# A retention and soft mixture-of-experts kernel on one core: the running maximum as a 129th column, a dispatch split in two, two scalings moved to GpSimd, and two more steps of k turned on the chip

## The chip, the cores and the metric

The kernel runs on one core of a Trainium2 chip. The metric is the device time of one execution in microseconds (us). An engine's work is named as in the profile: PE (TensorE, with PEld for its weight loads), DVE (VectorE), ACT (ScalarE), POOL (GpSimd), SP (SyncE, which issues all the DMAs here).

## The reference

Two layers follow each other. The first is a retention: per batch and head a 64x64 state decays by a factor of the head in each step of time and takes in k times v; the output is q times the state. The second is a soft mixture of 8 experts with 4 slots each: every slot takes a softmax over all 3072 tokens (dispatch), passes a two-layer network, and every token takes a softmax over the 32 slots (combine).

```python
for t in range(S):                                  # S = 768, 4 batches x 8 heads, head_dim 64
    state = gamma * state + k[t] outer v[t]
    y[t] = scale * (q[t] @ state)
x = y, as (3072 tokens, 512)
logits = x @ phi                                    # (3072, 32)
d = exp(logits - logits.max(0)); d /= d.sum(0) + 1e-9
slot_input = d.T @ x                                # (32, 512)
for e in range(8):
    h = maximum(slot_input[e] @ w1[e], 0)           # w1: 512 x 1024
    slot_out[e] = h @ w2[e]                         # w2: 1024 x 512
c = exp(logits - logits.max(1)); c /= c.sum(1) + 1e-9
out = c @ slot_out                                  # (3072, 512)
```

Everything is float32.

## The kernel before

**Attention in passes.** The sequence is cut into 6 chunks of 128 tokens; with 4 batches that makes 24 steps (`NSTEP`), step i being chunk i // 4 of batch i % 4. The loop at L437 makes 12 passes P of two steps each (`NPP`). A pass multiplies the carried state by q (`carry_mm`), the masked scores by v (`attend_mm`), copies the outputs out of PSUM (`attend_copy`), updates the state with k times v (`state_mm`, `state_add`), transposes the outputs to tokens x channels (`natural_mm`, `natural_copy`, the tile `xn`), and makes scores and masks of the next two steps (`score_mm`, `score_mask`). GpSimd multiplies the decays into q and v (`decay_q`, `decay_v`).

**Two layouts of k.** The scores need k with channels on the partitions, the state needs it with tokens on the partitions. The host lays down both, and a step's transfer brings kT, qT, v and the second layout of k, 1024 KB in all. For steps in `TURNED` (L46) and for the last four, the transfer stops ahead of the second layout (768 KB, L194), and for those in `TURNED` TensorE makes it by four transposes into bank A0, which ScalarE copies to the step's buffer (`turn_k`, L198 to L202; called at L487). A step of an even pass (P = 4) also has `turn_mm` and `turn_copy` of the dispatch behind it; a step of an odd pass has a dispatch and the logits.

**Dispatch by groups.** Four steps make a group g, one chunk of all batches, 6 groups in all. The logits of a group go to one PSUM bank "sm" as 128 partitions (4 batches x 32 slots) by 128 tokens (`logits_mm`). A running softmax over the tokens follows (`logits`): the maximum `m` so far, its negative `nm`, the exponentials `pT` with their sum `z`, and `al`, the factor by which what was summed before has to be scaled down. `pT` is transposed to `p`, and `dispatch_u` multiplies `p` by the `xn` of the group's four steps, into PSUM; `dispatch_acc` adds it to the accumulator `acc` (128 x 512) with the factor `al`, and `dispatch_z` does the same for the sums `zrun`.

**The turn to the experts** (L513 to L557) follows the last pass, in which the dispatch of group 4 (L475) and the first half of the logits of group 5 run ahead of `attend_mm`. Then: accumulate group 4, outputs and logits of the last steps, their maximum and exponentials (L522), the transposed `p` (L529), the factors `wj` that bring the four batches to one common maximum (L524 to L536, by way of a small matmul at L528), the dispatch of group 5 in two halves (L542), their accumulation, the division by the sums, and `siT`, the slots' inputs. `warm` (L409) multiplies zeros in the places where TensorE would wait. The first expert matmuls are those of L567.

**Order.** The order on every engine is the order of the code (`manual_schedule`). A wait for a buffer stands at its first writer.

**Buffers.** `ring` has 9 buffers of 512 KB: for the masked scores (two a pass), the transposed outputs and `xn` (one each a pass), and at P = 11 for four half-loads of w2 (L175). `inp` (6) holds the steps' inputs and `big` (13) weights; from P = 9 on weights go to `inp` too. All loads go through SyncE's one queue, and an issue whose buffer isn't free holds up the issues behind it. At L589 to L604 the last eleven weight loads are issued as the expert matmuls free buffers; the eight stores of L636 follow on the same queue.

**Experts.** `hidden` multiplies the slots' inputs by w1 (L567), L646 by w2 in three blocks of columns, and `finish` combines each block with the tokens' weights `cT` (L630), copies and stores it.

Of the kernel before, what the change touches and what calls it, by code (L numbers as in the profile page):

```python
# [11 lines left out]
AF = mybir.ActivationFunctionType  # L12
ALU = mybir.AluOpType
# [4 lines left out]
C = 128  # L18
# [24 lines left out]
NIN = 6  # L43
NRING = 9
PACE = (1, 1, 1, 2, 1, 2, 1, 2, 2, 0, 2, 2)
TURNED = (0, 1, 2, 3, 4, 8, 12)  # L46

K_MASK, K_VSC, K_YT = 0, 128, 176
K_ID, K_QT, K_GC, K_J, K_ALL = 272, 400, 496, 500, 504
# [32 lines left out]
def retention_soft_moe_kernel(  # L82
# [27 lines left out]
    def small(name, shape, bufs=1):  # L110
        return cpool.tile(shape, F32, name=name, bufs=bufs)

    def bank(name, shape=(128, 512)):
        return ps.tile(list(shape), F32, name=name)
# [190 lines left out]

    gs = {}

    def logits_mm(g, js):
        q = gs.setdefault(g, {})
        if "ltp" not in q:  # L310
            q["ltp"] = bank("sm", (128, C))
        for p in range(NPAIR):
            for j in js:
                nc.tensor.matmul(q["ltp"][32 * j:32 * j + 32, :], phis[:, p, :], st[GRP * g + j]["yT"][:, p, :],  # L314
                                 start=(p == 0), stop=(p == NPAIR - 1), skip_group_check=True,
                                 tile_position=(0, 32 * j))

    def logits(g):
        q = gs[g]
        lt = q["ltp"]  # L320
        q["pT"] = small("pT", [128, C])
        if g == NGRP - 1:
            nmx = small("nmx", [128, 1])
            nc.vector.tensor_reduce(nmx, lt, AX.X, ALU.max, negate=True)
            nc.vector.tensor_scalar(nmc[:, 1:2], nmx, nmc[:, 0:1], None, ALU.min)
            nc.scalar.activation(q["pT"], lt, AF.Exp, bias=nmc[:, 1:2], scale=1.0, accum_out=zc[:, 1:2])
            return
        nm = nmc[:, 0:1] if g == NGRP - 2 else small("nm", [128, 1])
        q["m"] = small("m", [128, 1], bufs=2)
        if g == 0:  # L330
            nc.vector.tensor_reduce(q["m"], lt, AX.X, ALU.max)
        else:
            mg = small("mg", [128, 1])
            nc.vector.tensor_reduce(mg, lt, AX.X, ALU.max)
            nc.vector.tensor_scalar(q["m"], mg, gs[g - 1]["m"], None, ALU.max)
        nc.vector.tensor_scalar(nm, q["m"], -1.0, None, ALU.mult)
        turn_l(g)
        q["z"] = zrun if g == 0 else small("z", [128, 1])
        nc.scalar.activation(q["pT"], lt, AF.Exp, bias=nm, scale=1.0, accum_out=q["z"])
        if g > 0:  # L340
            q["al"] = small("al", [128, 1])
            nc.scalar.activation(q["al"], gs[g - 1]["m"], AF.Exp, bias=nm, scale=1.0)

    def turn_l(g):
# [18 lines left out]
        q["p"] = small("pl", [128, C])  # L363
        nc.vector.tensor_copy(q["p"], pp)

    def dispatch_u(g, names):
        q = gs[g]
        q["up"] = [bank(n) for n in names]
        w = DM // len(names)
        for h, up in enumerate(q["up"]):  # L370
            for j in range(GRP):
                nc.tensor.matmul(up[32 * j:32 * j + 32, 0:w], q["p"][:, 32 * j:32 * j + 32],  # L372
                                 st[GRP * g + j]["xn"][:, h * w:(h + 1) * w], start=True, stop=True,
                                 skip_group_check=True, tile_position=(0, 32 * j))
# [2 lines left out]
        q = gs[g]  # L377
        nc.vector.scalar_tensor_tensor(zrun, zrun, q["al"], q["z"], ALU.mult, ALU.add)

    def dispatch_acc(g):  # L380
        q = gs[g]
        if g == 0:
            nc.scalar.copy(acc, q["up"][0])
            return
        w = DM // len(q["up"])
        for h, up in enumerate(q["up"]):
            a = acc[:, h * w:(h + 1) * w]
            nc.vector.scalar_tensor_tensor(a, a, q["al"], up[:, 0:w], ALU.mult, ALU.add)

    def combine_a(g):  # L390
        q = gs[g]
# [45 lines left out]
    for P in range(NPP):  # L437
# [34 lines left out]
            continue  # L472
        carry_mm(P)
        if last:
            dispatch_u(g - 1, ["A0"])  # L475
            logits_mm(g, (0, 1))
            load_halves(2)
            load_weights(2)
# [14 lines left out]
        if P % 2 == 1:  # L493
            if g > 0:
                dispatch_u(g - 1, ["S"])
            logits_mm(g, range(GRP))
            if g > 0:
                dispatch_acc(g - 1)
                combine_b(g - 1)
            if g > 1:  # L500
                dispatch_z(g - 1)
        score_mm(2 * P + 2)
        score_mask(2 * P + 2)
        score_mm(2 * P + 3)
# [7 lines left out]

    weight_pool[0] = big  # L513
    dispatch_z(g - 1)
    dispatch_acc(g - 1)
    attend_copy(NPP - 1)
    natural_mm(NPP - 1, (0,))
    combine_b(g - 1)
# [3 lines left out]
    logits(g)  # L522
    nj = small("nj", [128, GRP])
    nc.vector.tensor_scalar(nj, kt[:, K_J:K_J + GRP], nmc[:, 1:2], None, ALU.mult)  # L524
    natural_copy(NPP - 1, ("vector", "vector"), (1,))
    warm(2, "A0", 128)
    mb = bank("S", (128, GRP))
    nc.tensor.matmul(mb, rep, nj, start=True, stop=True)  # L528
    dispatch_p(g)  # L529
    al = gs[g]["al"] = small("al", [128, 1])  # L530
    nc.scalar.activation(al, gs[g - 1]["m"], AF.Exp, bias=nmc[:, 1:2], scale=1.0)
    warm(2, "A0", 128)
    nms = small("nms", [128, 1])
    nc.vector.tensor_reduce(nms, mb, AX.X, ALU.min)
    wj = small("wj", [128, 1])
    nc.scalar.activation(wj, nmc[:, 1:2], AF.Exp, bias=nms, scale=-1.0)  # L536
    gs[g]["z"] = zc[:, 1:2]
    dispatch_z(g)
    nc.vector.tensor_scalar(wsel, rep[:, 0:NSLOT], wj, None, ALU.mult)
    zw = small("zw", [128, 1])  # L540
    nc.vector.tensor_tensor(zw, zrun, wj, ALU.mult)
    dispatch_u(g, ["Y1", "A1"])  # L542
    dispatch_acc(g)
    zp = bank("S", (128, NSLOT))
    nc.tensor.matmul(zp, zw.broadcast_to([128, 128]), rep[:, 0:NSLOT], start=True, stop=True)
    sp = bank("A3", (128, NK * NSLOT)).rearrange("p (k s) -> p k s", s=NSLOT)
# [160 lines left out]
```

## Time and profile before

| | |
|---|---|
| median of three runs | 160.9 us (160.67 to 160.93) |
| the profiled execution | 160.49 us |
| its span, first to last instruction | 158.7 us |
| mean granted TensorE clock | 0.987 |
| DMA | 62.81 MB, of which 56.16 MB read and 6.29 MB written in HBM by the kernel's transfers |
| attention, to the end of the last `attend_mm` | about 101.7 us of the span |
| turn, to the first matmul of L567 | 101.7 to 107.9 us |
| experts and stores | 107.9 to 158.7 us |

The profile is of one execution. Its times run from the span's start. "The chain of waits" follows the work that ended last back from the end; a row of it gives start, length, engine, tile and line. A row of the timeline gives start and length of an instruction (or of several merged), its engine, line, what it writes and reads, and in brackets how long the engine had been idle and for whom it waited. A row of the windows gives a stretch, then busy time and count for PE, PEld, DVE, ACT and POOL, the granted clock, the DMA engines' mean busy share (1.00 is all 16), and GB/s. Rows of waits give the sum, the number of times and the longest. A DMA row gives the size and the time from issue to landing.

### The profile page before, as it was taken

What the parts mean: (1) busy time and instruction counts of PE and PEld (TensorE: products, weight loads), DVE (VectorE), ACT (ScalarE), POOL (GpSimd) and SP (SyncE); (2) the same over time, 40 slices, a digit from 0 to 9 for tenths busy, and PEclk for the clock granted to TensorE, in tenths of its full rate; (3) what the DMA queues carried; (4) which work ended last, traced back from release to release, by engine and by line L of the source; (5) the groups of instructions that cost most, each with busy time, mean ns of one, the idle gap of its engine ahead of it and who ended that gap; (6) DMA issues with size and microseconds to landing.
All of it is one profiled execution on the core that took longest, in us unless ns stands there. A gap on an engine that the chain in (4) does not pass through costs nothing.

```text
span 158.7 us, 5509 instructions
## 1 busy us (share of the span) xinstructions
PE 146.9 (93%) x2418; PEld 108.5 (68%) x2418; DVE 81.2 (51%) x201; ACT 39.8 (25%) x95; POOL 58.0 (37%) x62
## 2 busy tenths in 40 slices
PE   8899999999999999999999989999999999999700
PEld 2489989997998699979996867863233655556400
DVE  0347607592856385758574948488112304545510
ACT  3311552315142305130513051320101002424210
POOL 0352686965737377374738374000100000000000
PEclk9999999999999999999999999999999999999995
DMA  4999999999999999999999999999999999999991
GB/s 131 373 393 437 417 415 418 414 425 413 416 415 419 421 417 419 419 417 411 412 420 420 410 417 420 402 417 363 376 417 423 427 423 411 407 401 421 396 415 42
DMA packets 9816, 62.81 MB, mean 396 GB/s; under 512 B 1088, under 2 KB 1216, under 8 KB 4288
## 3 DMA queue, kind: packets, MB, share of 16 engines
q1 hardware_dynamic: 9792, 62.46, 96.4%
q8 instruction: 19, 0.31, 0.8%
q14 instruction: 5, 0.04, 0.1%
HBM read 56.16 MB, written 6.29 MB: 394 GB/s over the span
## 4 chain that ended last, share of the span: by engine, by line
PE 85%; DMA 3%; DVE 3%; issue 1%; ACT 1%; POOL 1%; SPq 0%; ACTq 0%; DVEq 0%
PE A L221 14%; PE Y L253 13%; PE A L646 9%; PE A L297 8%; PE S L281 6%; PE Y L244 6%; PE Y L567 4%; PE sm L314 4%; DMA r<-in_first_dram 3%; PE S L372 3%; PE A L567 2%; PE S L567 2%; PE A L630 2%; DVE r L228 2%; PE A L201 1%
## 5 line engine op out<-in xcount | busy, mean ns | idle before, releaser
L228 DVE TENSOR_TENSOR r<-A,kt 128x512 f32<-128x512 f32 x46 | 28.7, 684 | 18.8 <-PE A L221 18.8
L207 POOL TENSOR_TENSOR b<-b,qtab 128x512 f32<-128x512 f32 x20 | 25.5, 1276 | 24.5 <-DMA b<-in_x_dram 17.7
L221 PE MATMUL A<-b 64*128 64x128 f32 x384 | 25.2, 279 | 0.3 <-DMA b<-in_x_dram 0.3
L221 PEld LDWEIGHTS A<-b 64*128 64x128 f32 x384 | 22.5, 187 | 3.1 <-issue 2.2
L211 POOL TENSOR_TENSOR b<-b,kt 128x512 f32<-128x512 f32 x23 | 23.6, 1045 | 2.5 <-DMA b<-in_x_dram 2.5
L253 PE MATMUL Y<-r,b 128*64 128x128 f32 x352 | 22.3, 277 | 0.1
L253 PEld LDWEIGHTS Y<-r,b 128*64 128x64 f32 x352 | 19.0, 137 | 2.5 <-issue 2.3
L646 PE MATMUL A<-b,r 128*32 128x128 f32 (+1 forms) x352 | 15.9, 304 | 0.0
L646 PEld LDWEIGHTS A<-b,r 128*32 128x32 f32 x352 | 10.6, 110 | 7.1 <-issue 4.4
L304 ACT COPY r<-A 128x512 f32<-128x512 f32 x23 | 12.4, 591 | 9.4 <-PE A L297 9.4
L297 PE MATMUL A<-kt,r 128*128 128x128 f32 x96 | 13.2, 279 | 0.5 <-ACT r L272 0.5
L281 PE MATMUL S<-b 128*64 128x64 f32 x304 | 11.2, 222 | 0.8 <-issue 0.8
L297 PEld LDWEIGHTS A<-kt,r 128*128 128x128 f32 x96 | 10.4, 140 | 1.7 <-ACT r L272 0.7
L281 PEld LDWEIGHTS S<-b 128*64 128x64 f32 x304 | 10.6, 138 | 1.0 <-issue 1.0
L244 PE MATMUL Y<-b,sst 64*64 64x128 f32 x304 | 10.6, 276 | 0.0
L404 POOL TENSOR_TENSOR cn<-cn,cz 128x128 f32<-128x128 f32 x6 | 2.4, 399 | 20.4 <-DVE cz L403 14.9
L244 PEld LDWEIGHTS Y<-b,sst 64*64 64x64 f32 x304 | 8.2, 132 | 1.2
L273 DVE COPY r<-Y 128x512 f32<-128x512 f32 x9 | 6.2, 691 | 5.3 <-PE Y L253 4.5
L314 PEld LDWEIGHTS sm<-r,phis 128*32 128x32 f32 x192 | 6.2, 110 | 3.3 <-issue 3.3
L630 PE MATMUL A<-cT,r 32*128 32x384 f32 x26 | 8.3, 529 | 0.0
L567 PE MATMUL Y<-b,siT 128*32 128x512 f32 x64 | 8.2, 594 | 0.0
L290 DVE TENSOR_TENSOR sst<-sst,S 128x256 f32<-128x256 f32 x16 | 6.0, 417 | 3.1 <-PE S L281 3.1
(139 smaller groups left out, 177.8 us busy)
## 6 DMA issues: line engine op xcount, KB each, us to landing
b<-in_w_dram SPq DMA_DIRECT2D x30, 1024.0 KB, 14.7
b<-in_x_dram SPq DMA_DIRECT2D x13, 1024.0 KB, 12.5
b<-in_x_dram SPq DMA_DIRECT2D x10, 768.0 KB, 11.5
out_dram<-b SPq DMA_DIRECT2D x8, 768.0 KB, 9.0
r<-in_w_dram SPq DMA_DIRECT2D x4, 512.0 KB, 11.6
b<-in_x_dram SPq DMA_DIRECT2D x1, 512.0 KB, 4.3
r<-in_first_dram SPq DMA_DIRECT2D x1, 512.0 KB, 5.2
phis<-in_phi_dram SPq DMA_DIRECT2D x1, 64.0 KB, 9.4
```

The costliest lines, as they stand in the source:

```text
L207: nc.gpsimd.tensor_tensor(q, q, qtab, ALU.mult)
L211: nc.gpsimd.tensor_tensor(v, v, vsc[:, i // B, :].unsqueeze(2).broadcast_to([128, H, D]), ALU.mult)
L221: nc.tensor.matmul(s["sc"][r][:, g, :], s["kT"][half(r), g, :], s["qT"][half(r), g, :], start=True, stop=True, skip_group_check=True)
L228: nc.vector.tensor_tensor(s["A"][:, r], s["sc"][r], mask.unsqueeze(1).broadcast_to([128, NPAIR, C]), ALU.mult)
L244: nc.tensor.matmul(p["y"][k][b][half(half_of(r, g)), gl, :], sst[(2 * P + k) % B][half(r), g, :], s["qT"][half(r), g, :], start=(gl == 0 a ...
L253: nc.tensor.matmul(pr[P]["y"][k][g // 2][half(half_of(r, g)), g % 2, :], s["v"][:, 2 * g + r, :], s["A"][:, r, g, :], start=(P < B // 2 an ...
L281: nc.tensor.matmul(S_[half(r), k, g, :], s["kn"][:, 2 * g + r, :], s["v"][:, 2 * g + r, :], start=True, stop=True, skip_group_check=True)
L297: nc.tensor.transpose(X[k][:, g * 128:(g + 1) * 128], pr[P]["yT"][:, k, g, :], ident)
L304: (nc.scalar.copy if engines[k] == "scalar" else nc.vector.tensor_copy)(xn, pr[P]["X"][k])
L314: nc.tensor.matmul(q["ltp"][32 * j:32 * j + 32, :], phis[:, p, :], st[GRP * g + j]["yT"][:, p, :], start=(p == 0), stop=(p == NPAIR - 1), ...
L567: nc.tensor.matmul(hp[g][hf][32 * j:32 * j + 32, :], siT[:, k, :], w1t[4 * g + j, k][:, hf * 512:(hf + 1) * 512], start=(k == 0), stop=(k ...
L646: nc.tensor.matmul(op[32 * j:32 * j + 32, :w], hT[fc // 4][:, fc % 4, 4 * g + j, :], w2t[4 * g + j, cb, fc], start=(g == 0 and fc == 0), s ...
```

## The change

- `TURNED` also holds steps 10 and 16. Their transfers are 256 KB shorter each, and `turn_k` runs for them in passes 4 and 7.
- The logits' bank of the last group gets a 129th column, into which VectorE copies the running maximum `m` of group 4, in pass 10 (`logits_bank`). One reduction over 129 columns then gives the negative overall maximum `nmc[:, 1:2]`; the separate minimum goes.
- The dispatch of group 4 is split by columns: half 0 stays at its place in the last pass, half 1 stands in the turn, behind the copy of the last step's `xn`, where two products with zeros stood. Its accumulation is split likewise, the second part behind `dispatch_z(g)`.
- The last `natural_copy` goes from VectorE to ScalarE; `al` of the last group is computed earlier, and has two buffers.
- The second `warm` of the turn writes bank A2 in place of A0.
- `wsel` and `zw`, the scalings by `wj`, go from VectorE to GpSimd.

```diff
-TURNED = (0, 1, 2, 3, 4, 8, 12)
+TURNED = (0, 1, 2, 3, 4, 8, 10, 12, 16)
...
+    def logits_bank(g):
+        gs.setdefault(g, {})["ltm"] = bank("sm", (128, C + 1))
+        gs[g]["ltp"] = gs[g]["ltm"][:, 0:C]
+        if g == NGRP - 1:
+            nc.vector.tensor_copy(gs[g]["ltm"][:, C:C + 1], gs[g - 1]["m"])
...
-            nmx = small("nmx", [128, 1])
-            nc.vector.tensor_reduce(nmx, lt, AX.X, ALU.max, negate=True)
-            nc.vector.tensor_scalar(nmc[:, 1:2], nmx, nmc[:, 0:1], None, ALU.min)
+            nc.vector.tensor_reduce(nmc[:, 1:2], q["ltm"], AX.X, ALU.max, negate=True)
...
-    def dispatch_u(g, names):
+    def dispatch_u(g, names, hs=None):
...
-        for h, up in enumerate(q["up"]):
+        for h in range(len(names)) if hs is None else hs:
+            up = q.setdefault("up", {})[h] = bank(names[h])
...
         if last:
-            dispatch_u(g - 1, ["A0"])
+            dispatch_u(g - 1, ["A0", "A0"], (0,))
             logits_mm(g, (0, 1))
...
+        if P == NPP - 2:
+            logits_bank(NGRP - 1)
         score_mm(2 * P + 2)
...
     dispatch_z(g - 1)
-    dispatch_acc(g - 1)
+    dispatch_acc(g - 1, 2, (0,))
...
-    natural_copy(NPP - 1, ("vector", "vector"), (1,))
-    warm(2, "A0", 128)
+    al = gs[g]["al"] = small("al", [128, 1], 2)
+    nc.scalar.activation(al, gs[g - 1]["m"], AF.Exp, bias=nmc[:, 1:2], scale=1.0)
+    natural_copy(NPP - 1, ks=(1,))
+    dispatch_u(g - 1, ["A0", "A0"], (1,))
     mb = bank("S", (128, GRP))
     nc.tensor.matmul(mb, rep, nj, start=True, stop=True)
     dispatch_p(g)
-    al = gs[g]["al"] = small("al", [128, 1])
-    nc.scalar.activation(al, gs[g - 1]["m"], AF.Exp, bias=nmc[:, 1:2], scale=1.0)
-    warm(2, "A0", 128)
+    warm(2, "A2", 128)
...
     dispatch_z(g)
-    nc.vector.tensor_scalar(wsel, rep[:, 0:NSLOT], wj, None, ALU.mult)
+    dispatch_acc(g - 1, 2, (1,))
+    nc.gpsimd.tensor_scalar(wsel, rep[:, 0:NSLOT], wj, None, ALU.mult)
     zw = small("zw", [128, 1])
-    nc.vector.tensor_tensor(zw, zrun, wj, ALU.mult)
+    nc.gpsimd.tensor_tensor(zw, zrun, wj, ALU.mult)
     dispatch_u(g, ["Y1", "A1"])
-    dispatch_acc(g)
+    dispatch_acc(g, 2)
```

More of the change, by code (lines that the diff above doesn't have):

```diff
@@ L310, in logits_mm @@
         if "ltp" not in q:
-            q["ltp"] = bank("sm", (128, C))
+            logits_bank(g)
         for p in range(NPAIR):
@@ L340, in logits @@
         if g > 0:
-            q["al"] = small("al", [128, 1])
+            q["al"] = small("al", [128, 1], 2)
             nc.scalar.activation(q["al"], gs[g - 1]["m"], AF.Exp, bias=nm, scale=1.0)
@@ L364, in dispatch_p @@
         nc.vector.tensor_copy(q["p"], pp)
-    def dispatch_u(g, names):
+    def dispatch_u(g, names, hs=None):
         q = gs[g]
-        q["up"] = [bank(n) for n in names]
         w = DM // len(names)
-        for h, up in enumerate(q["up"]):
+        for h in range(len(names)) if hs is None else hs:
+            up = q.setdefault("up", {})[h] = bank(names[h])
             for j in range(GRP):
@@ L378, in dispatch_z, with dispatch_acc @@
         nc.vector.scalar_tensor_tensor(zrun, zrun, q["al"], q["z"], ALU.mult, ALU.add)
-    def dispatch_acc(g):
+    def dispatch_acc(g, n=1, hs=None):
         q = gs[g]
@@ L384, in dispatch_acc @@
             return
-        w = DM // len(q["up"])
-        for h, up in enumerate(q["up"]):
+        w = DM // n
+        for h in range(n) if hs is None else hs:
             a = acc[:, h * w:(h + 1) * w]
-            nc.vector.scalar_tensor_tensor(a, a, q["al"], up[:, 0:w], ALU.mult, ALU.add)
+            nc.vector.scalar_tensor_tensor(a, a, q["al"], q["up"][h][:, 0:w], ALU.mult, ALU.add)
     def combine_a(g):
```

## The prediction

> **What bounds the kernel now.** I read the chain of waits first, then SyncE's waits, then windows of half a microsecond over the two places where the DMA share sags, then the landing times of single transfers.
>
> ```profile
> PE 146.9 (93%) x2418; PEld 108.5 (68%) x2418; DVE 81.2 (51%) x201; ACT 39.8 (25%) x95; POOL 58.0 (37%) x62
> DMA  4999999999999999999999999999999999999991
> ...
> SPq L162 <- PE Y L567: 10.2, 4, 7.8
> ...
> SPq L702 <- DMA out_dram<-b: 5.7, 1, 5.7
> ```
>
> Two things are full at once: TensorE 93% of the span, and the DMA engines in every slice from the second to the last but one. The chain names PE almost throughout and no DMA after the first load. But after the last instruction of the computation SyncE waits another 5.7 us for the last store. So the last transfer ends the run, and the question is what fixes its time. The next fences give issue and landing of three transfers, each from a window that holds one issue.
>
> ```profile
> 101.73 0.33 SPq L162 DMA_DIRECT2D b<-in_w_dram  x1
> b<-in_w_dram SPq DMA_DIRECT2D x1, 1024.0 KB, 11.8
> 109.88 0.33 SPq L162 DMA_DIRECT2D b<-in_w_dram  x1
> b<-in_w_dram SPq DMA_DIRECT2D x1, 1024.0 KB, 6.1
> 151.55 0.33 SPq L636 DMA_DIRECT2D out_dram<-b  x1
> out_dram<-b SPq DMA_DIRECT2D x1, 768.0 KB, 6.1
> ```
>
> The last load before the turn lands at 101.73 + 11.8 = 113.5, the first one after it at 109.88 + 6.1 = 116.0, and the last store at 157.6, 1.1 before the end of the span. A transfer has landed when the slowest of the 16 engines is done, and at 417 GB/s (the usual rate of the GB/s row) 1024 KB take 2.5 us: 113.5 to 116.0 is just that. So the **slowest engine** goes from old to new load without a gap, although SyncE stood 7.8 us in between (its wait on Y L567, the first expert matmuls, which free weight buffers).
>
> ```profile
> 109.50:110.00 0.50, 0.50 (x8) 0.13 (x4) 0.36 (x1) 0.00 (x0) 0.00 (x0) 1.00 0.75 311
> 110.00:110.50 0.50, 0.50 (x8) 0.13 (x4) 0.48 (x1) 0.00 (x0) 0.00 (x0) 1.00 0.52 213
> ...
> 111.50:112.00 0.50, 0.50 (x12) 0.14 (x7) 0.00 (x0) 0.00 (x0) 0.37 (x1) 1.00 0.80 295
> 112.00:112.50 0.50, 0.50 (x8) 0.13 (x4) 0.31 (x1) 0.00 (x0) 0.03 (x1) 1.00 1.07 426
> ...
> 154.50:155.00 0.50, 0.00 (x0) 0.00 (x0) 0.00 (x0) 0.00 (x0) 0.00 (x0) 0.50 0.72 295
> 155.00:155.50 0.50, 0.00 (x0) 0.00 (x0) 0.00 (x0) 0.00 (x0) 0.00 (x0) 0.50 0.30 123
> ...
> 156.50:157.00 0.50, 0.00 (x0) 0.00 (x0) 0.00 (x0) 0.00 (x0) 0.00 (x0) 0.50 0.06 25
> ```
>
> The last two figures of a row are DMA share and GB/s. From 109.5 to 112 half of the engines are empty: they are ahead, ran dry, and wait for the issue at 109.88, whose data is flowing at about 111.7 (shares 0.80, then 1.07). At the end most engines stop near 155.0, and from 156 the share is 0.06, one engine of 16: it alone carries the end from 155.1 to 157.6, and nothing in the views shows it idle before. Its time is the sum of its bytes; the others' end hangs on when the weight buffers come free.
>
> **The change part by part.** *Two more steps turned.* Steps 10 and 16 load 768 instead of 1024 KB: 512 KB less in all, 512/1024 x 2.5 = **1.25 us** less for each engine, the slowest included, long before 113.5. In return TensorE transposes four blocks for each. A pass with a turned step against one without:
>
> ```profile
> 35.27 0.59 PE A L201 x4
> 35.86 0.87 PE A L297 x8
> ...
> 44.45 1.02 PE A L297 x8
> ...
> 97.90 1.00 PE A L372 x8
> 98.89 0.86 PE sm L314 x16
> ...
> 103.82 0.53 PE A L412 x4
> ...
> 105.37 0.49 PE Y L372 x8
> 105.86 0.43 PE A L372 x8
> 106.29 0.34 PE S L545 x2
> ```
>
> 0.59 + 0.87 - 1.02 = 0.44 us each, on the PE chain without cover: **+0.88 us**. (ScalarE's copy of a turned step, some 0.6 us, must leave bank A0 before the next scores: they follow the L201 by 0.87 us and more, so nothing.)
>
> *Half a dispatch.* The dispatch of group 4 at L475 takes 1.00 us for 512 columns; a half of 256 takes 0.43 to 0.49, say 0.46: -0.54. The other half takes the place of a warm-up of 0.53: -0.07. Together **-0.61 us**, if PE stays the path. It does: the last attends need masks that are done at 98.4, and the warm-up left in place covers exp, copy and minimum as before.
>
> *129th column.* L325 (0.21) goes.
>
> ```profile
> 95.21 0.28 ACT L357 COPY pl<-sm 128x128 f32<-128x128 f32 x1
> 95.88 2.48 DVE L228 TENSOR_TENSOR r<-A,kt 128x512 f32<-128x512 f32 x4 [2.16 <-PE A L221]
> ...
> 103.61 0.21 DVE L325 TENSOR_SCALAR nmc<-nmx,nmc 128x1 f32<-128x1 f32 x1
> 103.92 0.37 ACT L326 ACTIVATE pT<-sm,nmc 128x128 f32<-128x128 f32 x1 [1.00 <-PE A L297]
> 104.00 0.68 DVE L304 COPY r<-A 128x512 f32<-128x512 f32 x1
> 105.27 0.29 ACT L536 ACTIVATE wj<-nmc,nms 128x1 f32<-128x1 f32 x1 [0.71 <-DVE nms L534]
> ```
>
> Exp may start some 0.25 earlier, but TensorE runs fillers until 104.35, so it is worth nothing on the path. Its price is the copy of the maximum into the bank, of L325's size, on VectorE: it waits for L357 (until 95.49) and has 0.39 us before the masks at 95.88; if it is late, the masks' end at 98.4 still has over a microsecond before the attends at 99.75. Behind it on VectorE stand only these masks. Nothing.
>
> *Copy of step 23 to ScalarE.* Behind exp (from 103.92) and the moved `al` it would end near 105.1, less the 0.25: before the last dispatch at 105.37 and before wj at 105.27. Nothing. VectorE gives the 0.68 to the half accumulation, which stands before wj's users and ends before the first half of the last dispatch.
>
> *Scalings on GpSimd.* No row shows this operation.
>
> ```profile
> L404 POOL TENSOR_TENSOR cn<-cn,cz 128x128 f32<-128x128 f32 x6 | 2.4, 399 | 20.4 <-DVE cz L403 14.9 <-DVE zc L378 5.5
> L211 POOL TENSOR_TENSOR r<-r 128x512 f32<-128x512 f32 x1 | 1.5, 1547 | 6.0 <-DMA r<-in_first_dram 6.0
> L456 POOL COPY rep<-kt 32x128 f32<-32x128 f32 x4 | 1.1, 286 | 0.1
> L695 POOL MEMSET const-float32-0.0<- 128x1 f32 x1 | 0.1, 98 | 0.2 <-issue 0.2
> ```
>
> wj ends at 105.56, and TensorE is free for L545, which needs zw, at 106.29: 0.73 us for two operations and their hand-overs. Lowest 2 x 0.10, nearest 0.29 + 0.10 (128x32 and 128x1 are smaller than L404 and of L456's order), highest the first L211, twice: 3.1. I take 0.4 to 0.5 with hand-overs: covered, at most 0.1 on the path. The upper end is the slower rival below. [...]
>
> *Ring buffers.* The half held back keeps the two copies of group 4 until about 104.
>
> ```profile
> SPq L175 <- PE A L372: 3.7, 1, 3.7
> 98.92 0.33 SPq L175 DMA_DIRECT2D r<-in_w_dram  x1
> ```
>
> The fourth half-load waited for exactly that dispatch. Three buffers are free earlier; the next one in the order of the code is that of pair 10's outputs, free after L314 (99.75, less 0.54). So this issue moves by about 0.3, and those behind it on SyncE little, since they wait for the attends anyway. If instead it waited for the held half, 2.5 MB would come 5 us late; the slowest engine, busy until about 106 with what is queued, would lose some 0.9 of the 1.25.
>
> **The sum.** TensorE reaches the experts 0.88 - 0.61 = 0.27 us later, up to 0.4 with GpSimd. New data flows at 111.7 + 0.3 = 112.0; the slowest engine has finished old work at 113.5 - 1.25 = 112.25. It still has no gap, so all of the 1.25 should arrive at the end; the margin of 0.25 is thin, and I take **-1.2 us**. The next limit would be the others, 155.1 + 0.3 = 155.4, still below 157.6 - 1.2 = 156.4. The profiled execution took 160.49 with a span of 158.7; it becomes 159.3 with 157.5. The median of the three runs, 160.9, lies 0.4 above it: **159.7**.
>
> **The rivals.**
> *Only the restart counts* (0.16). If the end hangs on the release of weight buffers alone, the bytes saved before it only lengthen the hole at 110, and the time moves with TensorE: +0.3, 161.2. For it: half the engines do run dry there. Against it: 113.5 and 116.0 with no gap. The laggard is made by something, and the trace has 19 packets of instructions on a queue of their own:
>
> ```profile
> q8 instruction: 19, 0.31, 0.8%
> ```
>
> [...]
> *GpSimd becomes the path* (0.14, the slower side). Place: L545 and L548 behind wsel and zw. It turns the sign once the pair costs more than 0.73 + 1.5 = 2.2, since that much is swallowed first by the cover and then by the 1.5 us between 113.5 and 112.0. At the highest row, 3.1, TensorE is 0.3 + 2.4 = 2.7 late and the end 2.7 - 1.8 = 0.9 later: 161.8.
> *The turn isn't shorter* (0.12): the held half or a ring buffer gives back the 0.6, or the fourth half-load waits. TensorE 0.9 late, or the engine 0.9 idle: 0.3 to 0.9 gained, 160.3.
> *The laggard vanishes* (0.06): another engine fetches the instructions late; then the others' limit counts, -2.2: 158.7.
>
> **How the numbers follow.** The forecast has 0.52. Faster by over 0.2% (0.32 us, about what a measurement of this kernel can tell from none): 0.52 + 0.12 + 0.06 = 0.70. Only the restart is 0.11 within and 0.05 beyond; with GpSimd slower is 0.19. The range leaves out the vanished laggard and the dear GpSimd pair, 0.20: from 159.1 (forecast, less the lower runs and noise of 0.3 to 0.6) to 161.3 (restart alone).
>
> **What would show it.** Right: the last load before the turn lands about 1.25 after less queue (near 112.3), the first after it 2.5 later, the hole at 110 wider, one engine still alone at the end, last store landing near 156.4; L201 in passes 4 and 7, L372 of 0.46 twice, first L567 at about 108.2. Wrong: the last load at 112 and the next at 116 or later (restart), L545 waiting for GpSimd, L175's last issue after 104, or TensorE waiting for a bank at the second half dispatch.

## The result and the profile after

| | before | after |
|---|---|---|
| median (5 runs each, side by side) | 160.67 us | 162.55 us (161.91 to 163.19) |
| ratio, 95% interval | | 1.0121 [1.0081, 1.0161] |
| the profiled execution, its span | 160.49, 158.7 | 161.91, 160.1 |
| first expert matmul starts | 108.07 | 110.37 |
| from there to the end of the span | 50.6 | 49.8 |
| last store issued, landed | 151.55, 157.6 | 153.85, 159.0 |

The forecast was 159.7 (159.1 to 161.3), faster; it is 1.9 us slower. From a kernel's runs the comparisons leave out those more than 1.5% above its fastest as disturbed, and the profiled execution of the run called e5 below is one of these and isn't read.

Two rows of the page of after, TensorE and the DMA share in 40 slices:

```profile
PE 147.5 (92%) x2430; PEld 109.2 (68%) x2430; DVE 81.0 (51%) x199; ACT 41.2 (26%) x98; POOL 58.5 (37%) x64
...
DMA  4999999999999999999999978999899999999992
```

TensorE has more to do and a smaller share; the DMA engines, without a gap before, sag at the slices 24, 25 and 29.

In the profiled executions the end moves by 1.4: TensorE reaches the experts 2.3 us later, where 0.27 was forecast, and 0.9 of it comes back behind. First the chain of waits of after (start, length, what). It covers the two turned steps of passes 4 and 7, the turn, and a kind of row that the prediction did not use: "issue", time in which the engine waits for nothing that the profile shows.

```profile
44.49 0.59 PE A L201 x4
45.08 0.87 PE A L297 x8
...
51.73 0.77 issue
...
59.65 0.07 issue
...
69.54 0.59 PE A L201 x4
...
85.51 0.66 issue
...
93.01 0.79 issue
...
100.57 0.57 PE A L376 x8
...
106.06 0.57 PE A L376 x8
```

The same rows in the chain of before, with its first expert matmul:

```profile
51.37 0.55 issue
...
84.28 0.22 issue
...
108.07 0.93 PE A L567 x8
```

The turned steps and the two halves stand there as the change has them. What is new is 0.77 + 0.07 + 0.66 + 0.79 = 2.29 us of "issue" in the attention, against 0.55 + 0.22 = 0.77 before: **1.5 of the 2.3**. The turned steps add 0.88, the shorter turn takes 0.37, and some 0.3 is left to waits between engines in the last passes.

What these gaps are shows in the timeline of TensorE in after, around the one at 85.5, and in the DMA view of the stretch 83.5 to 84.0 (a queue, its packets and MB):

```profile
84.70 0.80 PE L281 MATMUL S<-b 128*64 128x64 f32 x21
86.17 0.56 PE L281 MATMUL S<-b 128*64 128x64 f32 x11 [0.66 <-issue]
...
q8 instruction: 1, 0.02, 13.5%
```

A run of 32 equal matmuls of `state_mm` is torn after the 21st. Nothing in these lines of the code asks for a stop there. Counted through TensorE's instructions in the trace, weight loads included, the gaps of before stand at number 1729 and 3009, those of after at 1729, 1985, 3009 and 3265: all are 193 + 256k, though the code at a number is another in part. The same holds for every gap over 0.1 us of the runs below, those in which the code is moved against the count included. Ahead of each lies one packet of 16 KB on queue q8, the kind "instruction" (19 of them, 0.31 MB, in the page of before). In after one starts at 83.72 and takes 1.08 us; TensorE goes on 1.4 us behind its end, at 86.17. So TensorE's program comes in **blocks of 256 instructions**, and at these places the next block isn't there yet. A block lasts 5.7 to 7 us in the attention. The fetch of the next block starts only some 3 to 5 us after the end of the block ahead, that is, after TensorE has entered the block in hand (in after 4.7, 4.9, 5.0 and 5.2 us at the four with gaps), so that with 1.1 for the packet and 1.4 behind it the block is just on hand or just not.

The DMA engines lose too. Windows of after (last two figures: share, GB/s), then two waits and three issues of SyncE, each issue with its row of size and time to landing:

```profile
92.00:94.00 2.00, 1.21 (x31) 0.79 (x25) 1.93 (x7) 0.00 (x0) 1.92 (x3) 1.00 0.79 324
94.00:96.00 2.00, 1.76 (x30) 1.52 (x27) 0.58 (x3) 1.23 (x4) 1.40 (x2) 1.00 0.68 201
96.00:98.00 2.00, 1.88 (x19) 1.47 (x21) 0.40 (x1) 1.07 (x3) 0.00 (x0) 1.00 0.83 299
...
112.00:114.00 2.00, 2.00 (x24) 0.62 (x20) 1.57 (x5) 0.00 (x0) 0.06 (x1) 1.00 0.69 205
```
```profile
SPq L159 <- PE Y L253: 7.7, 1, 7.7
...
SPq L175 <- PE sm L320: 3.6, 1, 3.6
```
```profile
103.98 0.33 SPq L162 DMA_DIRECT2D b<-in_w_dram  x1
b<-in_w_dram SPq DMA_DIRECT2D x1, 1024.0 KB, 10.5
112.18 0.33 SPq L162 DMA_DIRECT2D b<-in_w_dram  x1
b<-in_w_dram SPq DMA_DIRECT2D x1, 1024.0 KB, 5.1
153.85 0.33 SPq L643 DMA_DIRECT2D out_dram<-b  x1
out_dram<-b SPq DMA_DIRECT2D x1, 768.0 KB, 5.2
```

The load that waits for `attend_mm` of pass 10 (L253) is issued at 94.86 in place of 92.18, and from 92 to 98 the share sags to 0.68; before it was 1.00 to 1.02 there. So the engines now run dry at two places. The last load ahead of the turn lands at 103.98 + 10.5 = 114.5, the next one at 112.18 + 5.1 = 117.3: 2.8 later, where 2.5 would be without a gap.

Of the two places the first costs more. The load issued at 86.80 still lands at 97.1 (10.3 us later); in before the same load was issued at 84.90 and landed at 98.5 (13.6 us later). So at 97 us after is 1.4 ahead, the saved bytes in full. At the last load ahead of the turn it is 0.9 behind (114.5 against 113.5): 2.3 us are lost there, and 0.3 at the turn.

### The profile page after: what moved, and what is told of

Read it like the earlier page. It is cut to its first block, busy times and chain, and to the rows that moved or that the text cites. A ratio compares the mean times of both kernels' runs of the same rounds, so it can differ in the third digit from the quotient of the medians.

```text
span 160.1 us, 5542 instructions
## 1 busy us (share of the span) xinstructions
PE 147.5 (92%) x2430; PEld 109.2 (68%) x2430; DVE 81.0 (51%) x199; ACT 41.2 (26%) x98; POOL 58.5 (37%) x64
## 4 chain that ended last, share of the span: by engine, by line
PE 87%; DMA 3%; issue 2%; DVE 1%; POOL 1%; ACT 1%; SPq 0%; DVEq 0%
PE A L221 14%; PE Y L253 14%; PE A L653 9%; PE A L297 7%; PE Y L244 6%; PE S L281 6%; PE Y L574 4%; PE sm L320 4%; DMA r<-in_first_dram 3%; PE S L376 2%; PE A L574 2%; PE S L574 2%; PE A L201 2%; PE A L637 2%; PE sm L637 1%
## 5 line engine op out<-in xcount | busy, mean ns | idle before, releaser
L253 PE MATMUL Y<-r,b 128*64 128x128 f32 x352 | 22.6, 276 | 0.9 <-issue 0.8
L253 PEld LDWEIGHTS Y<-r,b 128*64 128x64 f32 x352 | 19.2, 137 | 3.4 <-issue 3.3
L304 ACT COPY r<-A 128x512 f32<-128x512 f32 x24 | 13.0, 592 | 8.2 <-PE A L297 8.2
L297 PEld LDWEIGHTS A<-kt,r 128*128 128x128 f32 x96 | 10.5, 140 | 1.7 <-ACT r L272 0.7
L320 PEld LDWEIGHTS sm<-r,phis 128*32 128x32 f32 x192 | 6.2, 110 | 2.9 <-issue 2.7
```

The source lines that it names most:

```text
L253: nc.tensor.matmul(pr[P]["y"][k][g // 2][half(half_of(r, g)), g % 2, :], s["v"][:, 2 * g + r, :], s["A"][:, r, g, :], start=(P < B // 2 an ...
L297: nc.tensor.transpose(X[k][:, g * 128:(g + 1) * 128], pr[P]["yT"][:, k, g, :], ident)
L304: (nc.scalar.copy if engines[k] == "scalar" else nc.vector.tensor_copy)(xn, pr[P]["X"][k])
```

## The experiments

All times are medians of all runs of a kernel. The ratio is to the kernel before, run beside it, whose medians lie between 160.46 and 160.78; where a text below takes differences of medians, a few tenths are within that scatter. "Idle" sums the pieces of "issue" over 0.06 us in the attention of the profiled execution, "experts" is the start of the first expert matmul there.

| run | what it is | us | ratio, 95% interval | idle | experts |
|---|---|---|---|---|---|
| before | | 160.67 | 1 | 0.77 | 108.07 |
| after | | 162.55 | 1.0121 [1.0081, 1.0161] | 2.29 | 110.37 |
| e1 | before + turned steps | 163.18 | 1.0155 [1.0115, 1.0195] | 2.68 | 111.41 |
| e2 | before + the rest | 160.39 | 0.9988 [0.9966, 1.0011] | 1.16 | 107.92 |
| e3 | after + 116 at the start | 160.94 | 1.0027 [0.9998, 1.0056] | 0.27 | 108.41 |
| e4 | after, 15 loads fewer | 157.13 | one run | 0 | 107.15 |
| e5 | before + 124 at the start | 160.67 | 1.0013 [0.9985, 1.0041] | | |
| e6 | e2 + 124 at the start | 160.44 | 0.9984 [0.9956, 1.0012] | 1.10 | 108.17 |
| e7 | e1 with whole loads | 163.47 | 1.0178 [1.0129, 1.0228] | 3.03 | 111.82 |
| e8 | before + 32 idle in passes 4, 7 | 162.68 | 1.0119 [1.0077, 1.0162] | 1.88 | 109.74 |
| e9 | before, 512 KB fewer | 160.39 | 0.9989 [0.9966, 1.0012] | 1.17 | 108.81 |
| e10 | before + 32 idle in the last pass | 160.79 | 1.0020 [0.9992, 1.0048] | 1.56 | 109.48 |
| e11 | e2 + step 6 turned | 162.15 | 1.0120 [1.0076, 1.0164] | 2.54 | 110.27 |
| e12 | after + 124 at the start | 160.94 | 0.9988 [0.9962, 1.0013] | 1.00 | 108.99 |
| e13 | after + 240 at the start | 161.80 | 1.0045 [1.0009, 1.0080] | 1.16 | 109.37 |
| e14 | before + 16 at the start | see there | 0.9954 [0.9916, 0.9992] | 1.51 | 108.59 |
| e15 | e2 + 512 KB fewer | 159.80 | 0.9953 [0.9933, 0.9974] | 1.17 | 108.44 |
| e16 | after + 64 at the start | 158.39 | 0.9878 [0.9846, 0.9910] | 0 | 107.02 |
| e17 | after + 184 at the start | 160.53 | 0.9985 [0.9956, 1.0015] | 0 | 107.99 |
| e18 | before + 64 at the start | 159.83 | 0.9960 [0.9939, 0.9980] | 0 | 107.35 |

The numbers "at the start" are TensorE instructions, four for each small product with zeros (16 of them take the pages' count of products from 2430 in after to 2462 in e16, and that of weight loads likewise), in the stretch where TensorE waits for the first loads anyway (its first product with data starts at 5.11 in before).

### Which half of the change, and is it the fetch (e1 to e4)

e1 is before with the new `TURNED` alone, e2 is after with the old one, e3 and e4 are after with one edit each:

```diff
 e3
-    warm(WARM)
+    warm(2)
+    warm(32, "sm", 8)
 e4, in the weight loads
-            t = large(weight_pool[0])
+            if which == "w1" and (e, k) != (0, 0):
+                t = one[0]
+            else:
+                t = large(weight_pool[0])
...
-                nc.sync.dma_start(t, w1[e // 2, k])
+                if (e, k) == (0, 0):
+                    one.append(t)
+                    nc.sync.dma_start(t, w1[e // 2, k])
```

> The kernel before with steps 10 and 16 turned and nothing else. Theory F (the 256-instruction blocks of TensorE come too late, because fetch and data share the DMA engines, and the added instructions bring TensorE to each block's end no earlier while the fetch gets slower): 0.88 us for the transposes and 1 to 2 us of added idle time at the block ends 1729, 3009 and 3265 of TensorE's instruction count, so the first L567 at 110 to 111 (before: 108.1) and 162 to 163.5 us. Rival T (the loss comes from the turn's edits: split dispatch, GpSimd, ring buffers): only the 0.88, L567 at 109.0, and with 512 KB less the time at 159.8 to 161.

> The changed kernel with the old list of turned steps: only the edits of the turn. Theory F: idle time of TensorE for its instructions as before (0.5 to 0.8 us in all in the attention), from the scores of steps 22 and 23 to the first expert matmul 12.9 us in place of 13.3, so that one 0.4 earlier, near 107.7; the bytes are those of before, so the lagging DMA engine ends as before and the time stays within 160.2 to 161.0, no gain over 0.4. Rival T: the first expert matmul at 109 or later and 161.5 to 162.5 us.

> The changed kernel, three of the five warm-up products of 256 columns at the start (while TensorE waits for the first load) replaced by 32 of 8 columns: 116 more instructions ahead of everything, the rest the same. Theory F: the idle times without a releaser leave the instructions at which they stood (L281 in passes 5 and 9, L253 in pass 10) and stand 116 instructions earlier in the code, again at counts 193 + 256 k of TensorE's instructions; the total stays within 161 to 163.5. Rival D (a dependency that the profile doesn't show, such as a late step's k or v): they stay at the same L281 and L253.

> The changed kernel with one load of w1 for all experts and rows (15 of the 32 weight loads are left out, and all experts multiply by the same block, so part of the computation is changed). The DMA engines then carry some 25 MB in the attention in place of 41. Theory F: the fetch of a block no longer stands behind data, its time from the previous block's end to ready falls from 6.3 to 7.6 us to under 6, and the idle times without a releaser fall from 2.3 to under 0.6 us: the first expert matmul at 108.3 to 108.9 in place of 110.4. Rival D: they stay, 110 or later.

The turned steps alone make the loss and more: 163.18. The whole turn (half dispatch, 129th column, GpSimd) costs nothing: e2 is 0.2 us below before, not told from zero, with 0.39 us more of idle time in its profiled execution, where as much as before was expected. The chain of e1, in time:

```profile
51.88 0.49 issue
...
59.53 0.34 issue
...
79.03 0.39 issue
86.17 0.67 issue
93.68 0.79 issue
```

Idle time of the same kind, at the counts 1729, 1985, 2753, 3009 and 3265. With 116 instructions more at an idle place (e3) nothing of the change is undone, yet the gaps at 51.7, 85.5 and 93.0 are gone, one of 0.27 at 68.6 is left, at number 2497, and 1.6 of the 1.9 us come back, though the start is 0.4 longer. The theory had expected them to move and to cost as much as before (161 to 163.5 us in all); rival D, gaps bound to lines of the code, falls with them. With fewer loads in the DMA engines' way (e4) a fetch waits 0.3 to 3.4 us and no gap is left. e3 touches the start and the place of the block ends. e4 takes traffic off all DMA engines (from 96 to 100 their share is 0.02 and 0.09, in before 1.00 and 1.01), so its 157.13 us need not be the gaps' alone; whether loads that TensorE waits for came earlier was not shown.

### Extra work, extra bytes or place (e5 to e8)

e5 and e6 put `warm(4)` and `warm(32, "sm", 8)` in place of `warm(WARM)` in before and in e2. e7 is e1, but steps 10 and 16 keep their whole loads. e8 is before with idle products where the turned steps would be:

```diff
 e7
-        elif i in TURNED or i >= NSTEP - B:
+        elif (i in TURNED and i not in (10, 16)) or i >= NSTEP - B:
 e8, behind turn_k in the loop of passes
+        elif P in (4, 7):
+            warm(4, "A0", 8)
```

> The kernel before with 32 warm-up products of 8 columns more and one of 256 less at the start, 124 instructions more ahead of everything. Theory F (idle time stands where a block of 256 TensorE instructions is used up before the next has come): other stretches of the code end the blocks, the idle time without a releaser in the attention falls from 0.77 us in the chain to 0.5 or less as it did in the padded changed kernel, the first expert matmul comes at 107.3 to 108.0 and the time is 159.8 to 160.6. Rival (the place of the blocks doesn't matter, the padded kernel won by chance): 160.3 to 160.9 with the idle times where they were.

> The edits of the turn alone (old list of turned steps), padded in the same way. Theory F: 0.3 to 0.5 us less idle in the attention and 0.4 less in the turn, the first expert matmul at 107.0 to 107.6. If the end follows the restart of the weight loads (theory R): 159.6 to 160.3, the fastest so far. If it follows a DMA engine that is never idle (theory L, that of the prediction): the bytes are those of before and it stays at 160.3 to 160.9.

> Steps 10 and 16 turned on the chip as in the change, but loaded whole: the bytes of before, the instructions of the change, the old turn. Theory F: the idle times come with TensorE's instructions and stay as with the turned steps alone (2.2 to 2.7 us in the chain), the first expert matmul at 110.5 to 111.5, 162.5 to 164. Rival B (the shorter transfers shift what the DMA engines do and make the fetches late): idle as before, 0.8, the first expert matmul at 109, 161 to 161.8.

> The kernel before with four products of zeros, 8 columns wide (16 instructions), in passes 4 and 7, in the places where the change turns steps 10 and 16: no data, no copy, about 0.25 us of TensorE time each. Theory F: the counts of the change with half its work: 0.5 us of work and 0.8 to 1.5 us more idle at block ends, the first expert matmul at 109.2 to 110, 161.3 to 162.5. Rival W (what costs is the transposes and their copies): 0.5 us, the first expert matmul at 108.5, 160.7 to 161.2.

e7 loses as much as e1, so saved bytes are not what hurts. e8 is the smallest edit that brings the loss: twice four products with zeros (eight matmul records, 0.28 us by its chain), make before as slow as the change.

```profile
44.51 0.28 PE A L412 x8
44.78 0.09 issue
...
51.57 0.67 issue
...
59.14 0.65 issue
...
78.70 0.47 issue
```

0.56 us of work and 1.1 us more of gaps make the first expert matmul 1.7 later; the median is 2.0 up. e5 and e6, moved by 124, don't change measurably against before. For both the theory expected less idle time, and for e5 a gain; e6 has 1.10 us of gaps, now at other places, and its first expert matmul at 108.17, so the move by 124 bought nothing there.

### Bytes alone, and instructions behind the gaps (e9 to e11)

e9 takes the 512 KB away without turning anything (steps 10 and 16 use v where they would use k, so the computation is another one). e10 puts eight idle products into the last pass, where few block ends follow. e11 adds step 6 to e2's `TURNED`, in pass 2, where the trace had the next block on hand over half a microsecond early:

```diff
 e9
-        elif i in TURNED or i >= NSTEP - B:
+        elif i in TURNED or i in (10, 16) or i >= NSTEP - B:
             nc.sync.dma_start(t[:, 0:1536], in_[i, :, 0:1536])
+            if i in (10, 16):
+                st[i]["kn"] = st[i]["v"]
 e10, behind the logits in the last pass
+            warm(8, "A3", 8)
 e11
-TURNED = (0, 1, 2, 3, 4, 8, 12)
+TURNED = (0, 1, 2, 3, 4, 6, 8, 12)
```

> The kernel before, with steps 10 and 16 loaded without the second layout of k (512 KB less) and nothing in its place: for these two steps the state takes v times v in place of k times v, so part of the computation is changed; TensorE's instructions are those of before. Theory L (the prediction's: the last store hangs on a DMA engine that is never idle, and bytes saved anywhere ahead come off the end): 1.0 to 1.3 us less, 159.2 to 159.6. Theory R (the last store hangs on when the weight buffers come free, and on the block fetches that one engine carries after that): 0 to 0.4 less, 160.1 to 160.6.

> The kernel before with the same 32 TensorE instructions as the dummies in passes 4 and 7, but all in the last pass, behind the first half of the logits, where a block of 256 lasts over 8 us. Theory F: half a microsecond of work and no idle time added, the first expert matmul at 108.4 to 108.7, 160.4 to 161.2. Rival (32 more instructions cost 2 us wherever they stand): 162 to 163.

> The edits of the turn with one more turned step, 6 in pass 2, where the next block was on hand some 0.8 us before it was needed. Theory F: 0.44 for the transposes, at most 0.3 more idle time, 0.4 less in the turn: the first expert matmul at 107.9 to 108.4 and 160.2 to 161.0. If the place of the turned step didn't matter: half of the two steps' loss, first expert matmul at 109, 161.3 to 162.

e9: half a megabyte less is worth 0.2 us with an interval that reaches zero, not 1.25. e10: the same instructions cost 0.1 us in the last pass (0.3 by the ratio), as expected, but its trace doesn't show that it is for want of gaps. Up to the last pass e10 is the kernel before, and yet its profiled execution has 0.79 more idle time than that of before, all ahead of the added products, and the first expert matmul at 109.48, not at 108.4 to 108.7 and hardly earlier than e8's 109.74. What tells the two executions apart is the first load behind the turn. It is issued at 111.55 in e8 and at 111.29 in e10 and takes

```profile
b<-in_w_dram SPq DMA_DIRECT2D x1, 1024.0 KB, 7.1
```
```profile
b<-in_w_dram SPq DMA_DIRECT2D x1, 1024.0 KB, 4.9
```

so that it lands 4.7 us behind the load ahead of it in e8 (114.0) and 2.7 behind it in e10 (113.4). The two executions end 2.0 us apart; why the load takes 7.1 us in e8 is not seen. e8 against e10 is therefore no proof that the gaps make the loss; the moved kernels below are the better one.

e11 fell: a turned step at a place with slack cost 1.8 us against e2. Its gaps (0.93, 0.34, 0.67, 0.60) stand at later blocks, at 51.8, 59.9, 85.8 and 93.4. From here on the theory says that what an insertion does is not decided where it stands: it moves every later block end against the rhythm of passes and loads. The next runs test that form.

### The place of the block ends (e12, e13, e14)

e12 and e13 are after with 124 and 240 more at the start, e14 is before with 16 more.

> The changed kernel with 124 TensorE instructions more at the start (four wide warm-up products kept, so that the start isn't slower as it was with two). Theory S (what costs is where the ends of the 256-instruction blocks fall in the code, and the change moved them by 9 and 18 instructions to a bad place): little idle time as in the first padded kernel, the first expert matmul at 107.6 to 108.3, 160.0 to 160.7, no slower than before. Rival C (the added instructions themselves bring the idle time, whatever their place): 161.3 to 162.5.

> The changed kernel with 240 instructions more at the start, 256 less 16, so that the block ends fall again within a few instructions of where they fell before the change in the code of passes 7 to 10. Theory S: idle time as before, 0.8 to 1.2 us in the chain, the first expert matmul at 108.2 to 109, 160.4 to 161.3. Rival C: 161.5 to 163.

> The kernel before with 16 TensorE instructions more at the start (four products of 8 columns, while TensorE waits for the first load anyway): no work added on the path, all block ends moved by 16. Theory S: 0.8 to 1.5 us more idle time at the ends, the first expert matmul at 108.8 to 109.6, 161.2 to 162.3. Rival C: nothing, 160.3 to 160.9.

e12 is 1.6 us below after with 124 instructions more, so instructions as such don't cost; eight of its twelve runs, those of its ratio, lie at 159.9 to 161.1, the other four at 162.5 to 164.3, and its 1.00 us of gaps is more than was expected. e13 gains 0.75, scatters from 160.4 to 163.1, and its median lies where rival C had it. e14 doesn't decide: five of its runs lie at 159.58 to 160.33 and six at 162.14 to 163.20 (one more, at 359, is no measure of anything), its ratio is of the lower five, and the profiled execution is of the lower one, with gaps of 0.71 and 0.80. The granted clock is the same in both groups (0.971 to 0.990 and 0.974 to 0.990). Whether the upper ones are gaps was not seen.

### What the change is worth without the gaps (e15 to e18)

e15 is e2 with e9's shorter loads, so both things that the forecast counted on without the turned steps' work (and e9's other computation). e16, e17 and e18 shift the blocks:

```diff
 e16 (after) and e18 (before), behind warm(WARM)
+    warm(16, "sm", 8)
 e17 (after)
-    warm(WARM)
+    warm(4)
+    warm(47, "sm", 8)
```

> The edits of the turn, and steps 10 and 16 loaded without the second layout of k and not turned (for them the state takes v times v in place of k times v, so part of the computation is changed): TensorE's path shortened by 0.4 and 512 KB less, none of the transposes. If both limits of the end stand close together (L and R), taking both back shows what either alone did not: 0.4 to 1.0 us less than before, 159.6 to 160.2. If the bytes are worth nothing: 160.3 to 160.7 like the turn alone.

> The changed kernel with 64 TensorE instructions more at the start. Theory S: some other idle time, between that of the changed kernel (2.3 us in the chain) and of the two padded ones (0.3 and 1.0); the time follows the first expert matmul: 160.2 if that comes at 108.2, 162 if at 110.

> The changed kernel with 184 TensorE instructions more at the start. Theory S: as for 64, another place of the block ends, another idle time; 160.2 if the first expert matmul comes at 108.2, 162 if at 110. If all three moves (64, 124, 184) come out below the changed kernel's 162.5, its place was a bad one of many; if two of them are as slow, 124 was a good one.

> The kernel before with the same 64 TensorE instructions more at its start that took the changed kernel from 162.55 to 158.39 us. If the gain was that of the change, set free from its stalls, the 64 do for the kernel before no more than take away its own 0.77 us of waits at block ends: between 159.6 and 160.7, so the changed kernel with them stays 1.2 us or more below. If the gain was that of the 64 (their place of the block ends lets the fetches come early, whatever the code), the kernel before with them falls as far, to 158.2 to 158.9, and the change is worth under 0.5 us at equal luck with the blocks. In the trace: the idle time at TensorE's counts 193+256k in the attention, and the first expert matmul (107.92 in the kernel before, 106.89 in the changed one with 64 more).

**e16 beats both kernels: 158.39 us, 1.2% below before**, with all of the change in it. In the three kernels with 64 or 184 more, no gap is left in the attention. A fetch starts 2.1 to 3.1 us (e16), 2.0 to 2.8 (e17) and 2.3 to 2.9 (e18) after the end of the block ahead, over blocks 3 to 12; in before it is 3.3 to 4.8, in after 3.3 to 5.2. e17's longer start costs it 1 us at once: the first `score_mm` starts at 6.88 in place of e16's 5.91. And e17, without a gap and with its first expert matmul at 107.99 where before has it at 108.07, is no faster than before (0.9985, an interval on both sides of 1). Before moved by 184 was not run.

e18 splits e16's gain. The 64 instructions are worth 0.8 us to before, and the change another 1.44 us (159.83 to 158.39; 158.28 to 159.03 in 4 runs against 159.47 to 160.62 in 12). As a ratio 0.9878/0.9960 = 0.992, with the two intervals added in squares 0.988 to 0.996. How it comes about shows in the three DMAs that carried the prediction, in e16 and then in e18:

```profile
100.63 1.02 SPq L162 DMA_DIRECT2D b<-in_w_dram  x1
b<-in_w_dram SPq DMA_DIRECT2D x1, 1024.0 KB, 11.5
108.83 0.33 SPq L162 DMA_DIRECT2D b<-in_w_dram  x1
b<-in_w_dram SPq DMA_DIRECT2D x1, 1024.0 KB, 5.8
150.50 0.33 SPq L644 DMA_DIRECT2D out_dram<-b  x1
out_dram<-b SPq DMA_DIRECT2D x1, 768.0 KB, 5.1
```
```profile
101.03 0.63 SPq L162 DMA_DIRECT2D b<-in_w_dram  x1
b<-in_w_dram SPq DMA_DIRECT2D x1, 1024.0 KB, 12.5
109.16 0.33 SPq L162 DMA_DIRECT2D b<-in_w_dram  x1
b<-in_w_dram SPq DMA_DIRECT2D x1, 1024.0 KB, 6.9
150.83 0.33 SPq L637 DMA_DIRECT2D out_dram<-b  x1
out_dram<-b SPq DMA_DIRECT2D x1, 768.0 KB, 6.3
```

The last load ahead of the turn lands at 112.1 against 113.5, the next one 2.5 later in both (114.6, 116.1), the last store at 155.6 against 157.1: no gap at the turn, and 1.4 to 1.5 less from there to the end. TensorE, at the experts 0.33 earlier, would account for 0.3 alone. In e17 the last load ahead of the turn is this:

```profile
101.60 0.33 SPq L162 DMA_DIRECT2D b<-in_w_dram  x1
b<-in_w_dram SPq DMA_DIRECT2D x1, 1024.0 KB, 11.6
```

It lands at 113.2, 0.3 earlier than in before, with the same bytes saved as in e16. The windows over the turn in e16 have the wider hole that was forecast; in e18 the shares of the first two are 0.98 and 0.92:

```profile
108.00:109.00 1.00, 1.00 (x12) 0.26 (x8) 0.84 (x2) 0.14 (x1) 0.00 (x0) 1.00 0.70 279
109.00:110.00 1.00, 1.00 (x16) 0.35 (x12) 1.00 (x2) 0.00 (x0) 0.00 (x0) 1.00 0.83 238
```

## Why the prediction was wrong, step by step

**The two turned steps: right.** The chain of after has 0.59 + 0.87 in both passes where 1.02 stood: 0.44 each, 0.88 together. In e16 and e18, which have no gaps, TensorE waits in pass 10 for ScalarE's copy of the outputs (L272, `attend_copy`), which stands behind the exponentials. The timeline of TensorE in e16 and in e18:

```profile
92.88 0.55 PE L297 MATMUL A<-kt,r 128*128 128x128 f32 x3 [0.83 <-ACT r L272]
```
```profile
92.77 0.65 PE L297 MATMUL A<-kt,r 128*128 128x128 f32 x4 [1.01 <-ACT r L272]
```

There e16 is only 0.11 later than e18, but that does not show the turned steps to be hidden. In e18's profiled execution two small operations of VectorE ahead of the masks (L402, L378) take 0.50 and 0.86 us, against 0.17 and 0.19 for the same two in e16, and 0.25 and 0.19 in before; why is not seen. The masks of e18 start at 88.15, and its `score_mm` stands 0.6 earlier than that of e16, whose masks start at 88.25. By an estimate from these rows e18 lost some 0.5 us there, and without it the change would reach the experts 0.2 later than e18, close to the 0.27 of the sum.

**The half dispatch: right in kind, mis-sized.** The sum took 0.46 for a half; it took 0.57 at both places. So 1.00 became 0.57, and a warm-up of 0.53 became 0.57: -0.39 in place of -0.61. From the last `score_mm` to the experts the turn went from 13.31 to 12.94 us, -0.37.

**129th column, ScalarE copy, GpSimd: right.** They cost nothing on the path; `wsel` took 0.36 us on GpSimd, `zw` 0.19, together from 107.94 to 108.45; the matmul that needs them starts at 108.51, as the dispatch ahead of it ends (108.56), so they are just covered, and the chain between 106 and 110 names TensorE alone. The rival in which GpSimd becomes the path has a time near the measured one and is wrong all the same: a time does not tell the cause.

**Ring buffers: right.** The fourth half-load waits 3.6 us at L175 as before, now for L320, the first half of the logits of group 5, as forecast. Counted from the start of the dispatch ahead, it is issued 0.5 later than in before (102.08 - 100.57 against 98.92 - 97.90), where the sum had 0.3.

**"TensorE reaches the experts 0.88 - 0.61 = 0.27 us later": this step failed.** It was 2.3. The sum added the durations of inserted instructions and had no term for what an insertion does to the instructions behind it. The trace had the warning: two rows of "issue" in the chain, 0.77 us, which the reading of the chain passed over, and the fetch packets, which it quoted, but only as what might make one DMA engine the slowest, not for whom they keep waiting. In their place the runs show 1.5 us more of waits for blocks. e8 shows that 32 idle instructions bring such waits too, e3, e12, e16 and e17 that moving the block ends takes away most or all of them, and with them 1.6 to 4.2 us.

**"All of the 1.25 should arrive at the end": failed too, and not only through the step ahead of it.** Up to 97 us the saved bytes come off as the sum has it: the load that lands at 98.5 in before lands at 97.0 to 97.2 in after, e9, e16 and e17. Whether they stay off is decided by the loads that wait for the last passes (from L159 at 92.18 on). The sum had no margin for these; it asked for a gap at the turn alone and found 0.25 us to spare there. In after they come 2.7 late, and 2.3 us are lost. In e9, with its first expert matmul 0.7 later, the last load ahead of the turn lands at 113.5 as in before, and 0.2 us is gained; in e15, 0.4 later, it lands at 113.1, and the gain is 0.75 (ratio 0.9953). A TensorE that is merely not late is not enough: e17 issues the first of these loads at 92.22, as before does, and keeps 0.3 of the saving. Only e16, at 91.26, keeps 1.4 to the last load (112.1) and to the end (1.44 against e18, beside -1.2 forecast). So the reasoning on the slowest engine holds in e16, where TensorE is 0.9 us earlier in the last passes, early enough for engines that have less to load; "it still has no gap" took that for granted. That the 0.9 us are the reason is argued from these runs, not tried by itself.

**Two readings of the windows were too strong.** From 155 to 156 the share is 0.30 and 0.15, so several engines are still at work, and one alone carries the end only from 156 on. From 110 to 112 the mean share is 0.79 rather than a half. The outcome does not hang on either.

**Shown and not shown.** Shown: the idle time stands at the ends of 256-instruction blocks, the fetch comes late there, and the same change is 1.9 us slower or, moved by 64 instructions, 2.3 us faster than before (2.0 by the ratio) and 1.4 faster than before moved likewise. Not shown: how far TensorE's delay goes into the time, which differs by up to 2 us for nearly the same delay (e8 and e10). Nor is it shown why a fetch waits 2 to 3 us with one place of the block ends and 3 to 5 with another. Places 64 and 184 are good, 0, 116, 124 and 240 worse; that is too few for a rule. The trace doesn't name the DMA engine that carries a packet, so what stands ahead of it is not seen. A load of 1024 KB, if it is spread evenly, gives each of 16 engines 64 KB, 2.5 us at 417 GB/s, so the waits are about one such share in the good kernels and up to two in the bad ones; that is an estimate from these numbers.

## What to carry to other kernels

Where every DMA engine is full (in before a share of 0.9 or more in 38 of 40 slices) and TensorE's program runs through thousands of instructions, look in the chain for "issue", and count TensorE's instructions there: in this case the gaps, a multiple of 256 apart (1729, 1985, 3009 and 3265 in after), were late fetches. An edit that adds or removes instructions moves all later ones, so measure it at two or three places (some idle instructions at the start, in both kernels) before you judge it; here the same change reads as +1.2% or, moved by 64 like the kernel it is compared with, as -0.8%. And work a gain through under the condition on which it rests, at every place where a load waits for a buffer: 1.25 us of DMA time were there to be had only in the kernel whose TensorE freed the buffers of the last passes 0.9 us earlier.

## What was not expected of the hardware

- A fetch of 256 TensorE instructions (16 KB) took 1.02 to 1.10 us on its DMA engine in the attention of before, started 2.0 us (e17) to 5.2 us (after) after the end of the block ahead while the loads ran, and TensorE went on 1.4 us behind its end (after, 84.80 to 86.17).
- 64 instructions at an idle place of the start made one kernel 4.2 us faster (after, 162.55 to 158.39) and the other 0.8 us (before, 160.67 to 159.83).
- 32 idle instructions of 0.56 us cost 2.0 us in passes 4 and 7 (e8) and 0.1 to 0.3 us in the last pass (e10).
- Gaps differ between executions of the same code: up to its last pass e10 is the kernel before, and its chain has 0.55, 0.13, 0.49 and 0.39 there, that of before 0.55 and 0.22. So of the 1.5 us between the idle times of after and before, some tenths are of the execution.
